# Weight pieces converted in pairs, and the first weight's blocks in two tiles

## The chip, the cores and the metric

The kernel runs on one core of a Trainium2 chip. The core has a matrix engine (TensorE, PE in the profile; PEld is its weight load), a vector engine (VectorE, DVE), a scalar engine (ScalarE, ACT), a general engine (GpSimd, POOL) and a queue engine that issues most transfers (SyncE, SP). Each works through its own instructions in order and waits on semaphores for the others. The metric is the time of one execution on the device in microseconds (us), the median of several runs.

## The reference

Attention without a softmax, normalised per head, then a two-layer feed-forward with a squared relu. The weights `w_in` and `w_out` arrive as 64-bit floats, everything else as 32-bit floats.

```python
kv  = einsum('bhsd,bhse->bhde', k, v)        # 8 x 8 heads, 576 positions, 64 wide
o   = einsum('bhsd,bhde->bhse', q, kv)
x   = o / sqrt(mean(o * o) + 1e-6) * g_norm  # -> (4608 tokens, 512)
r   = maximum(x @ w_in, 0.0)                 # w_in  (512, 2048)
out = (r * r) @ w_out                        # w_out (2048, 512)
```

## The kernel before

Tokens are worked in nine strips of 512. For each strip PE does the up product with `w_in`, then the down product with `w_out`; the attention of later tokens is woven in between. From strip 1 on the products use Strassen's scheme with seven block products (two levels of it further on), so sums and differences of blocks of the weights are needed. Blocks of `w_in` and their sums stay in SBUF; those of `w_out` go to DRAM (`w_out`, `w_deep`) and are streamed back. Only the first three blocks of `w_out` also lie in SBUF (`w_first`: 11, 21 and the sum t1).

The order of the work on each engine is written out by hand: the loop from line 1350 on runs through `steps` and calls transfers, conversions and slices of the attention (`slices`, `attend`) at fixed steps. What the engines are given is in program order, so work of DVE or ACT that is called earlier stands ahead on that engine.

**The conversion.** A weight arrives as 64-bit words and is turned into 32-bit floats with integer arithmetic. There are 32 pieces of 128 x 512 words (512 KB each): 16 of `w_in` (four quarters g, four row chunks kc) and 16 of `w_out`. For each piece ACT does two steps (`convert_on_act`: `w_c` from the upper half of the words, L254; the lower half in place, L258) and DVE four (`conversion`: L266, L268, L272, L275; the last writes the result). Pieces are taken two at a time (`convert_pieces`), the four DVE steps of the two interleaved. ACT is given the steps of the next two pieces before DVE's work on the present two. Then `load_more` has SP issue loads for buffers that come free: `raw` has eight buffers of one piece, `w_c` four.

- `pieces_in` puts pieces of `w_in` at their places; `pieces_out` puts the left half of `w_out`'s columns (blocks 11 and 21) into blocks 4 and 5 of the tile `w_in`.
- `sums_out` converts the right half into two `wt` tiles, which are further buffers of `raw`, forms four differences per tile (L317 to L323, by `minus`, L292) and issues two stores per tile to `w_out` in DRAM (L325), at once.
- `sums_in` scales a quarter on ACT (L301) and forms its block sums on DVE; this is called in the down product of strip 0, by when blocks 4 to 6 no longer hold `w_out`.

The tile `w_in` is [128, 2, 4, 7, 256]: row half, quarter, block, column. Blocks 0 to 3 are the quarters' own, 4 to 6 first `w_out`'s first blocks, later the sums of `w_in`.

**Strip 0.** The first quarter's four pieces are converted step by step between parts of the attention (`first_piece`, with one step on POOL). Then come 16 groups of `up_first` (g, fh, i): four products of 512 columns into one of four PSUM buffers, then a relu and two squares on ACT (L905, L907), which free the buffer. Three of the groups are multiplied early (`first_up`). Conversions are called between the groups: the two pieces with ids 4 and 5 behind group 0, and so on; the four calls of `sums_out` come at the steps 11, 13, 14 and 15. At step 14 blocks 11 and 21 are stored (`store_first`, L333). Then the 14 steps of the down product of strip 0 follow (`down`), which reads the blocks in `w_first`, then streams the others (L954). DVE's sums for it (L886), the normalisation of batch 1 (L490 to L505, L568), the deep sums of the weights (L995, L989) and `sums_in` share DVE; `combine` copies or adds a PSUM bank (L869, L1031) before the bank is used again.

Of the kernel before, what the change touches and what calls it, by code (L numbers as in the profile page):

```python
# [20 lines left out]
def kernel(  # L21
# [34 lines left out]
    nc = tc.nc  # L56
# [36 lines left out]
    raw_pool = conv.enter_context(tc.tile_pool(name="raw", bufs=8))  # L93
    spare_pool = conv.enter_context(tc.tile_pool(name="spare", bufs=1))
    wtmp = conv.enter_context(tc.tile_pool(name="wtmp", bufs=4))
# [113 lines left out]
    def drip_queries():  # L209
# [10 lines left out]
    w_in = wpool.tile([P, KH, NG, 7, WN // 2], FP32, name="w_in")  # L220
# [8 lines left out]
        w_in[:, :, :, b].rearrange("p k g e -> p (k g) e") for b in (4, 5, 6)  # L229
# [3 lines left out]
    sources = [w_in_v[kc, g] for g in range(NG) for kc in range(NP)]  # L233
    sources += [w_out_v[eh, j] for eh in range(2) for j in range(FQ)]
    raw = []

    def load_piece():
        if len(raw) < len(sources):
            t = raw_pool.tile([P, 2, WN // 2], I64, name="raw", tag="raw")
            nc.sync.dma_start(out=t, in_=sources[len(raw)])  # L240
            raw.append(t)
# [4 lines left out]
    words, acted = {}, [0]  # L246

    def convert_on_act(i, parts=(0, 1)):
        view = lambda dt: raw[i].bitcast(dt).rearrange("p b (n two) -> p b n two", two=2)
        low, high, high_f = view(U32)[:, :, :, 0], view(I32)[:, :, :, 1], view(FP32)[:, :, :, 1]  # L250
        r = view(I32)[:, :, :, 0]
        if 0 in parts:
            c = wtmp.tile([P, 2, WN // 2], FP32, name="w_c", tag="w_c")
            nc.scalar.activation(c, high_f, AF.Abs)  # L254
            words[i] = c, r, high

        if 1 in parts:
            nc.scalar.activation(r, low, AF.Copy, scale=2.0**-29)  # L258

    def conversion(i, dest, eng=nc.vector):  # L260

        c, r, high = words.pop(i)
        ci = c.bitcast(I32)


        yield eng.tensor_scalar(out=c, in0=c, scalar1=LEAST, scalar2=MOST, op0=ALU.max, op1=ALU.min)  # L266

        yield nc.vector.tensor_scalar(  # L268
            out=ci, in0=ci, scalar1=3, scalar2=0x3FFFFFFF, op0=ALU.logical_shift_left, op1=ALU.bitwise_and
        )  # L270

        yield nc.vector.scalar_tensor_tensor(  # L272
            out=ci, in0=high, scalar=-(2**30), in1=ci, op0=ALU.bitwise_and, op1=ALU.bitwise_or
        )
        yield nc.vector.tensor_tensor(out=dest.bitcast(I32), in0=ci, in1=r, op=ALU.add)  # L275

    def convert_pieces(ids, dests):

        for i in range(acted[0], min(ids[-1] + 3, len(sources))):
            convert_on_act(i)  # L280
            acted[0] = i + 1
        for _ in zip(*[conversion(i, dest) for i, dest in zip(ids, dests)]):
            pass
        load_more(ids[-1] + 1)
# [8 lines left out]

    def pieces_in(i):
        g, kc = divmod(i, NP)
        b = kc // KH * 2
        convert_pieces((i, i + 1), [w_in[:, kh, g, b : b + 2] for kh in range(KH)])

    def sums_in(g):

        nc.scalar.activation(w_in[:, :, g, 0:4], w_in[:, :, g, 0:4], AF.Copy, scale=g_col)  # L301
        a11, a21, a12, a22, s1, s2, s4 = (w_in[:, :, g, b] for b in range(7))
        nc.vector.tensor_tensor(out=s1, in0=a21, in1=a22, op=ALU.add)
        minus(nc.vector, s2, s1, a11)
        minus(nc.vector, s4, a12, s2)
        minus(nc.vector, a21, a11, a21)

    def pieces_out(j):
        dest = lambda j: w_in[:, j // NG, j % NG, 4:6]
        convert_pieces((NG * NP + j, NG * NP + j + 1), [dest(j), dest(j + 1)])  # L310

    def sums_out(j):
        js = (j, j + 1)
        t = [raw_pool.tile([P, 4, DH], FP32, name="wt", tag="raw") for _ in js]
        convert_pieces([NG * NP + FQ + j for j in js], [x[:, 0:2, :] for x in t])
        for x, j in zip(t, js):
            minus(nc.vector, w_out_t1[:, j, :], x[:, 0], w_out_11[:, j, :])  # L317
        for x, j in zip(t, js):
            minus(nc.vector, x[:, 2], x[:, 1], w_out_t1[:, j, :])
        for x in t:  # L320
            minus(nc.vector, x[:, 0], x[:, 1], x[:, 0])
        for x, j in zip(t, js):
            minus(nc.vector, x[:, 3], w_out_21[:, j, :], x[:, 2])  # L323
            for e in range(2):
                nc.sync.dma_start(out=w_out[3:7, :, e, j].rearrange("b p e -> p b e"), in_=x[:, :, ts(e, P)])  # L325
# [274 lines left out]
    def first_piece(i, n):  # L600

        if i not in first_steps:
            first_steps[i] = conversion(
                i, w_in[:, i % KH, 0, i // KH * 2 : i // KH * 2 + 2], nc.gpsimd if i else nc.vector
            )
        for _ in range(n):
            next(first_steps[i])
# [301 lines left out]
    def up(s, g, p):  # L909
# [5 lines left out]
        for i in range(2):  # L915
            product(p, i, lambda kc: w_in[:, kc, g, A_IN[p], ts(i, P)], lambda kc: rhs[:, :, kc, :], KH)
# [281 lines left out]
    w_half = lambda b, kc, f: w_in[:, kc, 2 * f : 2 * f + 2, b]  # L1198
# [148 lines left out]
    for i in range(NP, NP + 2):  # L1347
        convert_on_act(i)
    acted[0] = NP + 2
# [149 lines left out]
```

## Time and profile before

| | |
|---|---|
| median of 3 runs | 870.89 us (869.28 to 873.78) |
| profiled execution, span from first to last instruction | 867.8 us |
| median less that span | 3.1 us |
| PE busy | 858.3 us, 14176 matmuls |
| DVE busy | 721.5 us, 1236 instructions |
| ACT busy | 352.1 us, 805 instructions |
| POOL busy | 316.2 us, 321 instructions |
| granted clock of PE | 1.000 |

The span is that of the profiled execution; it is the only time of that execution which the page has. An engine's busy time counts instructions that are being carried out; matmuls are pipelined and the end of each is modelled, so a busy PE may have small holes. In a timeline a line gives start, length, engine, line of the code, operation, output and inputs with the shape, a count where several follow each other, and in brackets the idle time before it with the instruction or transfer that ended it.

### The profile page before, as it was taken

Reading aid. Unit: us, or ns where it says so; the run is one execution under the profiler, and the core shown is the slowest. Engines: PE = TensorE matmul, PEld = TensorE weight load, DVE = VectorE, ACT = ScalarE, POOL = GpSimd, SP = SyncE. Lnnn points to the kernel's source line nnn. Section 1 sums busy time; section 2 is a strip of 40 time slices with the busy share of each in tenths; the row PEclk is TensorE's granted clock in tenths of the full one; section 3 lists DMA queues with packets and bytes.
Section 4 is the critical chain, followed back from the end, with each engine's and each line's share of the span. In section 5 each row is a group of like instructions: output and inputs, shape, how many; then the busy total and the mean of one; then the engine's idle time right before and its main releaser. Section 6 shows DMA issues by size and latency. Waiting matters only on the chain.

```text
span 867.8 us, 32590 instructions
## 1 busy us (share of the span) xinstructions
PE 858.3 (99%) x14176; PEld 803.7 (93%) x14176; DVE 721.5 (83%) x1236; ACT 352.1 (41%) x805; POOL 316.2 (36%) x321
## 2 busy tenths in 40 slices
PE   8999999999999999999999999999999999999998
PEld 7445888889999999999999999999999999999998
DVE  3999998879887996789689977897889777975887
ACT  5799251320048303750356034901491148102810
POOL 1100003630459223730574045704470447145700
PEclk9999999999999999999999999999999999999999
DMA  9998997999999997989788979997668856885583
GB/s 312 301 335 251 288 376 233 296 323 361 276 261 261 346 328 235 232 311 336 213 244 272 336 244 258 294 317 260 213 221 300 305 161 220 291 286 195 177 311 124
DMA packets 169470, 236.47 MB, mean 273 GB/s; under 512 B 78704, under 2 KB 133744, under 8 KB 161008
## 3 DMA queue, kind: packets, MB, share of 16 engines
q1 hardware_dynamic: 169024, 234.33, 83.6%
q8 instruction: 111, 1.82, 0.9%
q14 instruction: 31, 0.25, 0.1%
q10 hardware_dynamic: 304, 0.07, 0.0%
HBM read 197.66 MB, written 36.70 MB: 270 GB/s over the span
## 4 chain that ended last, share of the span: by engine, by line
PE 83%; DVE 7%; ACT 5%; DMA 4%; issue 1%; SPq 0%; DVEq 0%; ACTq 0%
PE ps_A L854 35%; PE ps_B L854 31%; PE ps_C L854 5%; PE ps_A L859 4%; PE kv_ps L437 2%; PE x_ps L473 2%; PE ps_B L859 2%; DVE w_t L292 1%; ACT raw L258 1%; ACT w_c L254 1%; DMA w_blk<-w_deep 1%; DMA w_deep<-w_t 1%; DVE wt L292 1%; DMA first_qkv<-in_v_dram 1%; DMA raw<-in_moe_w_out_dram 1%
## 5 line engine op out<-in xcount | busy, mean ns | idle before, releaser
L854 PE MATMUL ps_B<-w_blk,g_s 128*64 128x128 f32 x2016 | 122.0, 273 | 0.0
L854 PEld LDWEIGHTS ps_B<-w_blk,g_s 128*64 128x64 f32 x2016 | 112.6, 137 | 0.1
L854 PE MATMUL ps_A<-x_l,w_in 128*64 128x128 f32 x1568 | 102.4, 273 | 0.6 <-ACT snap L1317 0.6
L292 POOL TENSOR_TENSOR x_l<-xT 128x256 f32<-128x256 f32 x21 | 16.0, 764 | 230.9 <-PE ps_A L854 230.9
L854 PE MATMUL ps_B<-w_blk,gt 128*64 128x128 f32 x1504 | 94.1, 273 | 0.9 <-DMA w_blk<-w_deep 0.9
L854 PE MATMUL ps_A<-w_blk,g_s 128*64 128x128 f32 x1536 | 92.2, 273 | 0.0
L854 PEld LDWEIGHTS ps_A<-x_l,w_in 128*64 128x64 f32 x1568 | 88.9, 137 | 0.9 <-ACT snap L1317 0.8
L1312 POOL TENSOR_TENSOR snap<-snap,gt 128x512 f32<-128x512 f32 x35 | 46.3, 1322 | 112.3 <-ACT snap L1317 102.7
L854 PEld LDWEIGHTS ps_B<-w_blk,gt 128*64 128x64 f32 x1504 | 84.6, 137 | 1.4 <-PE ps_B L854 1.1
L854 PEld LDWEIGHTS ps_A<-w_blk,g_s 128*64 128x64 f32 x1536 | 85.7, 137 | 0.0
L1317 ACT COPY snap<-ps_A 128x512 f32<-128x512 f32 x63 | 36.9, 585 | 103.8 <-PE ps_A L854 96.6
L1252 ACT ACTIVATE gt<-gt 128x512 f32<-128x512 f32 x112 | 70.1, 626 | 9.5 <-DVE gt L1312 9.5
L1253 ACT ACTIVATE gt<-gt 128x512 f32<-128x512 f32 x112 | 70.7, 631 | 3.6
L854 PE MATMUL ps_A<-w_blk,gt 128*64 128x128 f32 x1152 | 71.2, 273 | 0.0
L1101 ACT COPY o_sb<-ps_A 128x128 f32<-128x128 f32 x24 | 6.4, 266 | 144.9 <-PE ps_A L854 115.5
L854 PEld LDWEIGHTS ps_A<-w_blk,gt 128*64 128x64 f32 x1152 | 64.7, 137 | 0.0
L1100 DVE TENSOR_TENSOR o_sb<-o_sb,ps_B 128x256 f32<-128x256 f32 (+1 forms) x123 | 47.4, 386 | 15.0 <-ACT o_sb L1101 9.8
L292 DVE TENSOR_TENSOR gt<-gt 128x2048 f32<-128x2048 f32 (+1 forms) x29 | 59.7, 2063 | 0.0
L1312 POOL TENSOR_TENSOR gt<-gt,snap 128x512 f32<-128x512 f32 x42 | 52.6, 1283 | 15.0 <-DVE snap L1312 15.0
L854 PE MATMUL ps_B<-x_l,w_blk 128*64 128x128 f32 x784 | 51.2, 273 | 0.0
L854 PE MATMUL ps_A<-x_l,w_blk 128*64 128x128 f32 x784 | 51.2, 273 | 0.0
L1101 ACT COPY o_sb<-ps_B 128x128 f32<-128x128 f32 x31 | 8.3, 266 | 96.5 <-PE ps_B L854 96.5
(196 smaller groups left out, 1836.5 us busy)
## 6 DMA issues: line engine op xcount, KB each, us to landing
w_blk<-w_deep SPq DMA_DIRECT2D x56, 1024.0 KB, 7.4
w_blk<-w_out SPq DMA_DIRECT2D x56, 768.0 KB, 6.6
w_blk<-w_in_deep SPq DMA_DIRECT2D x49, 768.0 KB, 5.9
raw<-in_moe_w_in_dram SPq DMA_DIRECT2D x16, 512.0 KB, 7.4
raw<-in_moe_w_out_dram SPq DMA_DIRECT2D x16, 512.0 KB, 4.9
k<-in_k_dram SPq DMA_DIRECT2D x29, 256.0 KB, 5.4
v<-in_v_dram SPq DMA_DIRECT2D x29, 256.0 KB, 6.0
x_d<-x_q SPq DMA_DIRECT2D x27, 256.0 KB, 5.2
```

The lines of the kernel that those rows point to most:

```text
L254: nc.scalar.activation(c, high_f, AF.Abs)
L292: eng.tensor_tensor(out=out, in0=a, in1=b, op=ALU.subtract)
L437: nc.tensor.matmul(ps[ts(h, D), i], lhsT=a, rhs=w, start=i == 0 and c == 0, stop=c == C, skip_group_check=True)
L473: nc.tensor.matmul(ps[half, r, i, ts(p, D)], lhsT=q[row, half], rhs=kvd[b, p][row, row], start=True, stop=True)
L854: nc.tensor.matmul(ps[half], lhsT=lhsT[:, half], rhs=rhs, start=start, stop=stop, skip_group_check=True)
L859: nc.tensor.matmul(bank[BANK[p]][:, i, :], lhsT=lhsT(k), rhs=rhs(k), start=p in (1, 5, 2) and i == 0 and k == 0, stop=k == n - 1, skip_gro ...
L1100: add = lambda out, a, b: nc.vector.tensor_tensor(out=out, in0=a, in1=b, op=ALU.add)
L1101: yield nc.scalar.copy(q[:, 3:4], small(1))
L1252: nc.scalar.activation(o, o, AF.Relu)
L1253: nc.scalar.activation(o, o, AF.Square)
L1312: add = lambda eng, out, a, b: eng.tensor_tensor(out=out, in0=a, in1=b, op=ALU.add)
L1317: nc.scalar.copy(t, ps)
```

## The change

Two pieces that lie side by side share one buffer of `raw` and one of `w_c`, each twice as large and half as many, and every step of ACT and DVE takes both at once (128 x 1024). The first four pieces are still converted one by one, on halves of such buffers. So that the two pieces of a pair lie side by side in the result as well, the chunks of the quarters 1 to 3 are loaded in the order 0, 2, 1, 3. The tile `w_in` keeps four blocks per quarter; the other three, with `w_out`'s first blocks and later the sums, are a tile `w_s`, and `block(b)` chooses between them. `sums_out` uses one tile for two pieces, and its differences, two blocks at a time, and its stores come after the conversion of the following pair (`left_out`); the last two sets come together.

```diff
-    raw_pool = conv.enter_context(tc.tile_pool(name="raw", bufs=8))
+    raw_pool = conv.enter_context(tc.tile_pool(name="raw", bufs=4))
-    wtmp = conv.enter_context(tc.tile_pool(name="wtmp", bufs=4))
+    wtmp = conv.enter_context(tc.tile_pool(name="wtmp", bufs=2))
...
-    w_in = wpool.tile([P, KH, NG, 7, WN // 2], FP32, name="w_in")
+    w_in = wpool.tile([P, KH, NG, 4, WN // 2], FP32, name="w_in")
+    w_s = wpool.tile([P, KH, NG, 3, WN // 2], FP32, name="w_s")
+    block = lambda b: w_in[:, :, :, b] if b < 4 else w_s[:, :, :, b - 4]
...
-    sources = [w_in_v[kc, g] for g in range(NG) for kc in range(NP)]
+    sources = [w_in_v[kc, g] for g in range(NG) for kc in (range(NP) if g == 0 else (0, 2, 1, 3))]
...
     def load_piece():
-        if len(raw) < len(sources):
-            t = raw_pool.tile([P, 2, WN // 2], I64, name="raw", tag="raw")
-            nc.sync.dma_start(out=t, in_=sources[len(raw)])
+        i = len(raw)
+        if i < len(sources):
+            if i % 2 == 0:
+                raw_pairs.append(raw_pool.tile([P, 2, 2, WN // 2], I64, name="raw", tag="raw"))
+            t = raw_pairs[i // 2][:, i % 2]
+            nc.sync.dma_start(out=t, in_=sources[i])
             raw.append(t)
...
+    def act_words(c, view, parts=(0, 1)):
+        low, high_f, r = view(U32)[..., 0], view(FP32)[..., 1], view(I32)[..., 0]
+        if 0 in parts:
+            nc.scalar.activation(c, high_f, AF.Abs)
+        if 1 in parts:
+            nc.scalar.activation(r, low, AF.Copy, scale=2.0**-29)
...
+    def convert_pair_on_act(n):
+        view = lambda dt: raw_pairs[n].bitcast(dt).rearrange("p a b (n two) -> p a (b n) two", two=2)
+        c = wtmp.tile([P, 2, WN], FP32, name="w_c", tag="w_c")
+        act_words(c, view)
+        pair_words[n] = c, view(I32)[..., 0], view(I32)[..., 1]
...
-    def convert_pieces(ids, dests):
-
-        for i in range(acted[0], min(ids[-1] + 3, len(sources))):
-            convert_on_act(i)
+    def convert_pair(n, dest, add_eng=nc.vector):
+
+        for i in range(acted[0], min(n + 2, len(sources) // 2)):
+            convert_pair_on_act(i)
             acted[0] = i + 1
-        for _ in zip(*[conversion(i, dest) for i, dest in zip(ids, dests)]):
-            pass
-        load_more(ids[-1] + 1)
+        deque(conversion(pair_words.pop(n), dest, add_eng=add_eng), 0)
+        load_more(2 * n + 2)
...
     def pieces_in(i):
-        g, kc = divmod(i, NP)
-        b = kc // KH * 2
-        convert_pieces((i, i + 1), [w_in[:, kh, g, b : b + 2] for kh in range(KH)])
+        g, k = divmod(i // 2, KH)
+        convert_pair(i // 2, w_in[:, k, g].rearrange("p (a b) e -> p a (b e)", a=2))
...
     def pieces_out(j):
-        dest = lambda j: w_in[:, j // NG, j % NG, 4:6]
-        convert_pieces((NG * NP + j, NG * NP + j + 1), [dest(j), dest(j + 1)])
+        k, g = divmod(j, NG)
+        convert_pair((NG * NP + j) // 2, side(w_s[:, k, g : g + 2, 0:2]))
+
+    left_out = []
 
     def sums_out(j):
-        js = (j, j + 1)
-        t = [raw_pool.tile([P, 4, DH], FP32, name="wt", tag="raw") for _ in js]
-        convert_pieces([NG * NP + FQ + j for j in js], [x[:, 0:2, :] for x in t])
...
+        x = raw_pool.tile([P, 2, 4, DH], FP32, name="wt", tag="raw")
+        last = j + 2 == FQ
+        convert_pair((NG * NP + FQ + j) // 2, side(x[:, :, 0:2, :]), nc.vector)
+        left_out.append((x, slice(j, j + 2)))
+        while len(left_out) > (0 if last else 1):
+            left_sums(*left_out.pop(0))
+
+    def left_sums(x, js):
+        minus(nc.vector, w_out_t1[:, js, :], x[:, :, 0], w_out_11[:, js, :])
+        minus(nc.vector, x[:, :, 2], x[:, :, 1], w_out_t1[:, js, :])
+        minus(nc.vector, x[:, :, 0], x[:, :, 1], x[:, :, 0])
+        minus(nc.vector, x[:, :, 3], w_out_21[:, js, :], x[:, :, 2])
+        for i in range(2):
             for e in range(2):
-                nc.sync.dma_start(out=w_out[3:7, :, e, j].rearrange("b p e -> p b e"), in_=x[:, :, ts(e, P)])
+                nc.sync.dma_start(out=w_out[3:7, :, e, js.start + i].rearrange("b p e -> p b e"), in_=x[:, i, :, ts(e, P)])
...
-    for i in range(NP, NP + 2):
-        convert_on_act(i)
-    acted[0] = NP + 2
+    convert_pair_on_act(NP // 2)
+    acted[0] = NP // 2 + 1
```

The up product and the sums of `w_in` address their weights by `block(b)` in place of an index into `w_in`; nothing else there is altered.

## The prediction

> **What bounds the kernel now.** I read the page first, then busy time by stage, then the PE timeline, and the ACT and DVE timelines of the stage in which weights are converted (30 to 132 us; the conversion itself ends at 95.4).
>
> ```profile
> PE 858.3 (99%) x14176; PEld 803.7 (93%) x14176; DVE 721.5 (83%) x1236; ACT 352.1 (41%) x805; POOL 316.2 (36%) x321
> PE   8999999999999999999999999999999999999998
> DVE  3999998879887996789689977897889777975887
> ACT  5799251320048303750356034901491148102810
> DMA  9998997999999997989788979997668856885583
> ```
>
> PE is busy nearly everywhere. DVE is full only in slices 2 to 6 (22 to 130 us), ACT in slices 3 and 4, DMA through most of it.
>
> ```profile
> 40.00:50.00 10.00, 10.00 (x24) 4.38 (x24) 10.00 (x23) 9.26 (x19) 0.00 (x0) 1.00 1.11 315
> 50.00:60.00 10.00, 9.71 (x23) 3.94 (x22) 10.00 (x23) 9.56 (x21) 0.00 (x0) 1.00 1.03 377
> 60.00:70.00 10.00, 10.00 (x45) 4.77 (x44) 10.00 (x21) 9.87 (x22) 0.00 (x0) 1.00 0.72 251
> 80.00:95.40 15.40, 15.40 (x159) 11.83 (x158) 15.40 (x40) 8.64 (x20) 0.80 (x1) 1.00 1.04 305
> 95.40:131.80 36.40, 36.14 (x235) 31.31 (x233) 35.30 (x63) 12.78 (x15) 0.00 (x0) 1.00 0.97 340
> ```
>
> After the window come its length, then busy time of PE, PEld, DVE, ACT, POOL, the clock (1.00), DMA share and GB/s. PE, DVE, ACT and DMA are all close to full here: four resources side by side, each with little slack against the others. A busy PE may still be waiting, so I take gaps from start to start.
>
> ```profile
> 37.12 1.88 PE L900 MATMUL ps_A<-xT,w_in 128*128 128x512 f32 x4
> 39.22 1.98 PE L900 MATMUL ps_A<-xT,w_in 128*128 128x512 f32 x4 [0.22 <-DVE w_in L275]
> 51.34 3.60 PE L900 MATMUL ps_A<-xT,w_in 128*128 128x512 f32 x8
> 55.23 3.70 PE L900 MATMUL ps_B<-xT,w_in 128*128 128x512 f32 x8 [0.29 <-ACT gt L907]
> 131.80 7.17 PE L859 MATMUL ps_A<-w_blk,gt 128*128 128x256 f32 x32 [0.26 <-DVE o_sb L1031]
> ```
>
> Eight records take 3.43 us where nothing waits (0.429 each; one product is two). So 37.12 + 4 x 0.429 = 38.84 and the next start, 39.22, leaves 0.39 lost to weights not yet converted; 51.34 + 3.43 = 54.77, so 0.46 lost before 55.23 to ACT, which frees PSUM. Likewise 0.42 before 131.80 (DVE's o_sb), 0.30 before 70.77, and 0.11 to 0.21 at 58.77, 93.12 and 109.61. Together 2.0 us: all that PE can gain in this stage, however fast the other engines get.
>
> ```profile
> 46.92 0.69 ACT L254 ACTIVATE w_c<-raw 128x512 f32<-128x512 f32 x1
> 48.75 0.68 ACT L254 ACTIVATE w_c<-raw 128x512 f32<-128x512 f32 x1 [0.57 <-DMA raw<-in_moe_w_in_dram]
> 50.52 0.66 ACT L907 ACTIVATE gt<-ps_A 128x256 f32<-128x256 f32 x2
> 51.52 0.69 ACT L254 ACTIVATE w_c<-raw 128x512 f32<-128x512 f32 x1 [0.35 <-DMA raw<-in_moe_w_out_dram]
> ```
>
> ACT starts on piece 14 at 46.92 while piece 15 is still under way, and on piece 16 at 51.52; both waits end with a landing.
>
> ```profile
> 75.45 0.75 DVE L292 TENSOR_TENSOR wt<-w_in,wt 128x256 f32<-128x256 f32 x2
> 76.12 0.75 DVE L266 TENSOR_SCALAR w_c<-w_c 128x512 f32<-128x512 f32 x2
> 77.47 1.29 DVE L272 SCALAR_TENSOR_TENSOR w_c<-raw,w_c 128x512 int32<-128x512 int32 x2
> 95.42 2.49 DVE L886 TENSOR_TENSOR g_s<-gt 128x512 f32<-128x512 f32 x4
> ```
>
> Start to start, a 256-wide DVE operation costs 0.335 us and a 512-wide one 0.60; TENSOR_SCALAR at 512 costs 0.335.
>
> **Pairs on DVE.** From 0.335 and 0.60 the fixed part is 0.067 us. A 1024-wide operation is then 1.134; the one 2048-wide row, 2.20 us to the next start, lies on the line. TENSOR_SCALAR at 1024 has no row: 0.602 with the same fixed part, 0.67 if nothing is saved, 1.13 if the wider form ran at the others' rate. I take 0.602, as its operand stays contiguous. A pair is 2 x 0.602 + 2 x 1.134 = 3.47 us against 3.75: 0.28 less for each of 14 pairs, 3.9 us. The block sums go from 32 operations of 256 to 16 of 512, 16 x 0.067 = 1.1 us. DVE loses 5.0 us of work. If the far end (1.13) held, a pair would be 4.54 and the ten pairs before 69.7 would be 8 us late; I hold this unlikely.
>
> **Pairs on ACT.** A 512-wide conversion step costs 0.567 us start to start, the 2048-wide scaling 1.93; by that line 1024 costs 1.02, so 28 steps save 0.11 each, 3.2 us. But one step now needs both pieces landed. Piece 15 was issued at 40.62 and took 8.1 us, landing 48.7; piece 17, issued 45.03, took 7.6, landing 52.7. With DMA share at 1.03 to 1.11 these landings do not move. So pair 7 runs on ACT 48.75 to 50.77 instead of from 46.92 in parts, the group behind it (relu, two squares, 1.18 us) ends at 51.95 instead of 51.1, and PE's group of 51.34 starts at 52.2. Pair 8 starts at 52.75, its group ends at 55.95 against 55.1, and PE's 55.23 becomes 56.1. Pair 9 (landed by 55.2) starts at once. PE is 0.85 us late from here; nothing behind it gives that back but gaps that ACT had caused, some 0.1 to 0.3. Lower end: the landings come earlier by as much and ACT's saving of 1.1 us by then removes the 0.57 of gaps; upper end 1.5, if both pieces were late in turn.
>
> **The order of pieces.** From the second quarter on, a pair is row chunks 0 and 2, then 1 and 3. PE's second product of a group needs the second pair. At 37.12 that matters: pair 2 starts on DVE at 31.7, when its one ACT step is over, ends 35.2, pair 3 ends 38.7; PE stops after one product (37.98) until 38.8, so the gap is 0.83 instead of 0.39. This 0.44 is absorbed in the later start at 52.2. In the two later quarters conversion is done some 4 us before use; uncovered, each would cost up to 0.8.
>
> **Block sums one step later, four buffers.** The sums of a w_out pair and its four stores now follow the conversion of the next pair. The tile of the third pair takes the first one's buffer, so its last conversion step waits for those stores. By the rates above DVE is ready for pair 13 at 71.2, but its ACT step follows three relu groups and copies, as before at 72.2, so DVE starts at 73.1; conversion ends 76.6, the first sums 79.0 (before: 76.1 for these, 79.9 for that conversion). Stores then take, like those issued 75.90 to 77.47 and 82.33 to 83.92, 5.1 to 5.6 us from the first issue to the last landing: 84.2 to 84.7. Three conversion steps end at 81.3, so DVE stands 2.9 to 3.4 us, then needs 1.13 + 2.4 + 3.47 + 2.4 + 2.4: it ends at 96.6 instead of 95.4, 1.2 late. Queued behind it are g_s (PE needs it at 100.57, ready at 97.9: covered), x_n (1.4 us of slack before 104.03) and, through a DVE chain with 0.3 us of holes, o_sb at 131.06, which has no slack. On SP the 16 stores stay in number; the last go out 0.9 to 1.2 later, and the load that reads them (landed 106.4, used 109.6) has 3 us of cover.
>
> **Two tiles.** Strides change, sizes do not: nothing. DMA bytes and issue counts are equal.
>
> **Sum.** PE is 0.85 late by 56 and is held again at 131.8, where DVE's 1.2 lets it start 1.2 later than before. Not additive: about 1.2 with both, less 0.2 of small gaps, +1.0 us. The profiled span of 867.8 becomes 868.8; the 3.1 us between span and median stay, 871.9.
>
> Two sentences of the Trainium skill (Perfetto Trace Analysis, Optimizing Scalar/DVE Operations) pull in opposite directions here: grouping into larger operations can raise throughput on a saturated engine, and breaking instructions up lets work complete sooner where the engine only causes bubbles in others. By the first the time would be rival one's, by the second the forecast's; the rows at 48.75 and 131.80 bear out the second.
>
> **Rivals.** One: the saving carries through. Landings come early enough, the store wait stays under DVE's lead of 2.2 us, and PE closes its gaps: at most -2.0, time 869.0. For it: DVE is full for 65 us and o_sb is late. Against it: the two landings. Two, slower: the stores take the 8.1 us that the w_deep stores of 105 to 108 us took. The last one, issued at 80.65, lands at 88.75, DVE stands 7.4 us, ends 5.2 late, and o_sb passes it on: 875.9. It decides from a stand of 2.2 us on, one for one, and passes 0.5% at 6.6. For it: DMA share 1.04 in 80 to 95 us; against: stores of that very stage took 2.7 to 3.8 at the median. Three: the sums of two blocks are one strided write now; if PE's reads of neighbouring blocks at 83.76 were held for the last such write (96.6), 12.8 us are lost: 883.7. Against: DVE wrote one such block at 92.74 while a strided store of another, issued at 88.20 for 7.3 us, was still under way.
>
> **How the numbers follow.** Forecast 0.52, rival one 0.22, two 0.14, three 0.03, unnamed shifts of later loads (one load now costs PE 1.1 us at 288) 0.09. Half a percent, 4.35 us, is about what a measurement can tell from no change. PE's gaps forbid more than -2.0 here, so faster is 0.06 for unnamed causes; slower holds three, most of two and some unnamed, 0.17. The range runs from rival one less the runs' own scatter (868.4) to rival two (876.2). The forecast by itself spans 870.2 (the landings cost nothing, the stores do) to 873.6 (both ends of these costs). The three runs before span 4.5 us, which is more than the forecast's step.
>
> **What would show it.** Right: 128x1024 rows at 1.1 to 1.3 us on DVE, ACT pair steps at 48.75 and 52.75, PE starts at 52.2 and 56.1, and DVE idle about 3 us before the third L275 into wt, ended by a w_out store. Wrong: no such idle time, DVE's end before 94, or a PE gap near 84.

## The result, and the profile after

The changed kernel takes 875.39 us (median, 873.52 to 880.19) against 869.98 us (868.49 to 873.78) for the kernel before, run beside it: a ratio of 1.0062, with a 95% interval of 1.0047 to 1.0077. It is slower by 5.4 us. In its profiled execution the span is 872.5 us, 4.7 more than the 867.8 of before. Of the page of the changed kernel, busy time by engine and the rows by slice:

```profile
PE 859.9 (99%) x14176; PEld 804.5 (92%) x14176; DVE 719.6 (82%) x1164; ACT 349.2 (40%) x777; POOL 315.2 (36%) x321
PE   8999999999999999999999999999999999999998
DVE  3898999779967996889788976897889777875897
ACT  5779251230047502660357024911491147102810
DMA  9997998999999997989797979998677956885483
```

DVE carries out 72 instructions fewer and is busy for 1.9 us less, and ACT too does the same work in less time: read by busy time alone, the change is a small success. The windows of the same kernel (length; busy time of PE, PEld, DVE, ACT, POOL; clock, DMA share, GB/s) tell another story:

```profile
80.00:95.40 15.40, 15.40 (x158) 11.37 (x157) 11.95 (x16) 8.94 (x19) 0.10 (x1) 1.00 1.07 320
95.40:131.80 36.40, 33.88 (x224) 29.20 (x223) 35.29 (x63) 13.31 (x16) 0.00 (x0) 1.00 0.94 330
```

From 80 to 95.4 us DVE was busy without a break before; now it is idle for 3.45 us of them. In the window behind that PE is busy for 2.26 us less than before. The PE timeline of the changed kernel at its new holes:

```profile
39.42 2.84 PE L919 MATMUL ps_A<-xT,w_in 128*128 128x512 f32 x6 [1.73 <-DVE w_in L290]
53.05 3.70 PE L919 MATMUL ps_A<-xT,w_in 128*128 128x512 f32 x8 [0.48 <-ACT gt L926]
106.57 1.31 PE L662 MATMUL xt_ps<-ident,x_n 128*128 128x128 f32 x8 [0.90 <-DVE x_n L587]
114.03 2.21 PE L878 MATMUL ps_A<-w_blk,gt 128*128 128x256 f32 x9 [1.60 <-DVE gt L306]
136.09 7.17 PE L878 MATMUL ps_A<-w_blk,gt 128*128 128x256 f32 x32
```

(The lines of the code have moved: L281, L283, L287, L290 are the four steps that were L266, L268, L272, L275; L306 is `minus`, L926 the squares, L587 `x_n`, L878 the products of the down stage.) Taken from start to start as before, the holes are 1.89 us before 39.42, 0.65 before 53.05, 0.62 before 57.10, 1.06 before 106.57 and 1.8 before 114.03. The start that was at 131.80, where PE waited for DVE's `o_sb`, is at 136.09, just behind the same sum (135.35 to 136.03 on DVE). The ACT timeline of the changed kernel, at the steps that the prediction spoke of:

```profile
49.60 1.15 ACT L257 ACTIVATE w_c<-raw 128x1024 f32<-128x1024 f32 x1 [3.75 <-DMA raw<-in_moe_w_in_dram]
53.66 1.16 ACT L257 ACTIVATE w_c<-raw 128x1024 f32<-128x1024 f32 x1 [0.67 <-DMA raw<-in_moe_w_out_dram]
```

And the DVE timeline of the changed kernel, one whole pair, then the place where DVE stands, then its first sum for the down product:

```profile
39.28 0.69 DVE L281 TENSOR_SCALAR w_c<-w_c 128x1024 f32<-128x1024 f32 x1
40.00 0.69 DVE L283 TENSOR_SCALAR w_c<-w_c 128x1024 int32<-128x1024 int32 x1
40.73 1.23 DVE L287 SCALAR_TENSOR_TENSOR w_c<-raw,w_c 128x1024 int32<-128x1024 int32 x1
42.09 1.23 DVE L290 CUSTOM_DVE_ANT_0 w_in<-raw,w_c 128x2048 uint16<-128x2048 uint16 x1
43.23 0.69 DVE L281 TENSOR_SCALAR w_c<-w_c 128x1024 f32<-128x1024 f32 x1
...
82.79 1.23 DVE L287 SCALAR_TENSOR_TENSOR w_c<-raw,w_c 128x1024 int32<-128x1024 int32 x1
87.16 1.23 DVE L290 CUSTOM_DVE_ANT_0 wt<-raw,w_c 128x2048 uint16<-128x2048 uint16 x1 [3.14 <-DMA w_out<-wt]
...
99.85 2.49 DVE L905 TENSOR_TENSOR g_s<-gt 128x512 f32<-128x512 f32 x4
```

Two things are to be seen. A pair takes 39.28 to 43.23, 3.95 us, where the two pieces in turn took 3.75 before: the wide form is slower. And DVE stands for 3.14 us at 87.16 until the delayed stores have left the buffer. `g_s` starts at 99.85 instead of 95.42, 4.43 us later, and from there nothing is made up: `x_n` 105.83 (before 101.41), `o_sb` 135.35 (before 131.06), the first product of strip 1 on PE 143.10 (before 138.81), the end 4.7 later.

**Where the 4.43 us come from.** I cut DVE's time up to `g_s` in three, from PE's first wait for converted weights (24.86 before, 24.41 after; the profiles differ by up to 2.4 us in what lies ahead of it, so I count from there): up to the start of pair 3; from there to the start of pair 12, which is nine pairs; and the last four pairs with all sums and stores. Before, these are 11.08, 33.75 and 25.73 us; after, 10.91, 35.59 and 28.94. So -0.17, +1.84 (nine times 0.20) and +3.21 (3.14 of it is the stand), less 0.45 for the earlier opening: 4.43. The same cut serves for all experiments.

**PE's own lateness.** The early holes are less than that. Counted from the same wait, PE's first product with `gt` starts 58.90 us later before (83.76) and 60.83 after (85.24), so by then PE is 1.93 us late, while DVE is 4.88 late at `g_s` and strip 1 is 4.74 late. PE makes up the difference standing: it waits for DVE before 106.57 and 114.03.

### The profile page after: what moved, and what is told of

It is laid out like the page before. It is cut to its first block, busy times and chain, and to the rows that moved or that the text cites. A ratio compares the mean times of both kernels' runs of the same rounds, so it can differ in the third digit from the quotient of the medians.

```text
span 872.5 us, 32448 instructions
## 1 busy us (share of the span) xinstructions
PE 859.9 (99%) x14176; PEld 804.5 (92%) x14176; DVE 719.6 (82%) x1164; ACT 349.2 (40%) x777; POOL 315.2 (36%) x321
## 4 chain that ended last, share of the span: by engine, by line
PE 78%; DVE 10%; DMA 7%; ACT 3%; SPq 1%; issue 1%; DVEq 0%
PE ps_A L873 33%; PE ps_B L873 29%; PE ps_C L873 5%; PE ps_A L878 4%; DMA w_blk<-w_deep 3%; PE kv_ps L456 2%; PE x_ps L492 2%; PE ps_B L878 2%; DVE w_t L306 1%; DVE w_c L287 1%; DMA w_blk<-w_in_deep 1%; DMA w_blk<-w_out 1%; DVE wt L306 1%; DVE gt L306 1%; PE ps_C L878 1%
## 5 line engine op out<-in xcount | busy, mean ns | idle before, releaser
L306 POOL TENSOR_TENSOR x_l<-xT 128x256 f32<-128x256 f32 x21 | 16.3, 775 | 230.5 <-PE ps_A L873 230.5
L306 DVE TENSOR_TENSOR gt<-gt 128x2048 f32<-128x2048 f32 (+1 forms) x29 | 59.6, 2063 | 0.0
L873 PE MATMUL ps_A<-x_l,w_in 128*64 128x128 f32 x896 | 58.5, 273 | 0.0
L873 PEld LDWEIGHTS ps_A<-x_l,w_in 128*64 128x64 f32 x896 | 50.8, 137 | 0.1
```

Of the source, the lines that this page charges most:

```text
L306: eng.tensor_tensor(out=out, in0=a, in1=b, op=ALU.subtract)
L873: nc.tensor.matmul(ps[half], lhsT=lhsT[:, half], rhs=rhs, start=start, stop=stop, skip_group_check=True)
```

## The experiments

Theory: two DVE costs make up the loss, the slower wide step and the stand for the stores; ACT's pairs, the order and the two tiles cost nothing that lasts. Rival: the late landings, to which ACT's pairs are bound, hold PE from 53 us on, and DVE's part is hidden. A second question was why a wide step is slow: by its width or because each step reads what the one before wrote.

All times in us. "Pair 3", "nine pairs" and "last four" are the three stretches, "g_s" their sum against before, "strip 1" the first product of strip 1, counted from the same wait, against before (113.95). The ratio is that of medians to the kernel before, with its 95% interval. Single runs of one kernel differ by several us, so a place in a trace settles a delay better than a median does. Behind the start of strip 1 the profiled executions take between 729.0 us (before) and 735.5 (halves_in_turn), in no order that follows the edits (731.7 in split_alone); the cause stays open, and it may be why medians and places differ. The rows from the third on stand in the order of the sections below.

| kernel | pair 3 | nine pairs | last four | g_s | strip 1 | ratio |
|---|---|---|---|---|---|---|
| before | 11.08 | 33.75 | 25.73 | 0 | 0 | 1 |
| after | 10.91 | 35.59 | 28.94 | +4.88 | +4.74 | 1.0062 (1.0047 to 1.0077) |
| sums_at_once | 10.90 | 35.59 | 26.41 | +2.34 | +2.66 | 1.0042 (1.0022 to 1.0061) |
| halves_in_turn | 10.70 | 34.36 | 29.18 | +3.68 | +3.53 | 1.0062 (1.0038 to 1.0085) |
| both_undone | 10.70 | 35.51 | 25.61 | +1.26 | +3.34 | 1.0039 (1.0018 to 1.0060) |
| tiles_alone | 11.05 | 33.75 | 25.61 | -0.15 | +0.26 | 1.0020 (1.0003 to 1.0037) |
| delay_alone | 11.05 | 33.75 | 29.37 | +3.61 | +3.47 | 1.0051 (1.0033 to 1.0068) |
| wide_alone | 11.57 | 43.98 | 31.04 | +16.03 | +19.33 | 1.0226 (1.0202 to 1.0250) |
| act_and_order_undone | 11.57 | 43.96 | 35.31 | +20.28 | +20.16 | 1.0235 (1.0215 to 1.0256) |
| one_after_other | 11.20 | 42.37 | 29.53 | +12.54 | +12.41 | 1.0162 (1.0139 to 1.0186) |
| wide_new_order | 11.55 | 35.59 | 26.44 | +3.02 | +3.30 | 1.0052 (1.0032 to 1.0073) |
| act_undone | 11.55 | 35.59 | 29.78 | +6.36 | +6.24 | 1.0096 (1.0068 to 1.0124) |
| mixed | 11.06 | 33.75 | 28.53 | +2.78 | +3.18 | 1.0040 (1.0014 to 1.0066) |
| split_alone | 11.05 | 33.75 | 25.74 | -0.02 | +0.18 | 1.0000 (0.9982 to 1.0017) |

### The sums at once

The changed kernel, with the differences and stores of each pair right behind its conversion.

```diff
-        while len(left_out) > (0 if last else 1):
+        while left_out:
```

> The changed kernel, but the block sums of a w_out pair and its stores follow its own conversion at once. Theory (two costs on DVE: the wait of the third wt tile for the first one's stores, 3.0 us, and 0.2 us more per pair because a wide step waits for the one before it): the 3.1 us of idle time before the third L290 into wt goes, DVE ends its last block sum near 96.9 us instead of 99.9, and the time falls by 2.5 to 3.0 us against the changed kernel: ratio to before 1.0025 to 1.0035. Rival (the early holes of PE at 39, 53 and 57 us decide, DVE's late end is covered): no more than 0.5 us, ratio 1.0055 or above.

DVE doesn't stand for the stores any more and the last stretch falls from 28.94 to 26.41, 2.53 us less. It isn't back at 25.73: the first sum now reads what the last conversion step has just written and starts 1.26 us behind it (80.45 to 81.71) in place of 1.14, and the pairs are still slow. So the stand is a real cost of 2.5 us on the path to strip 1, where 2.1 us of it arrive. `g_s` comes at 97.44 and the ratio is 1.0042, both somewhat above what was expected.

### DVE's steps on the halves in turn

The changed kernel, but DVE takes each of the four steps on the first piece, then on the second, 512 wide.

```diff
-        deque(conversion(pair_words.pop(n), dest, add_eng=add_eng), 0)
+        of = pair_words.pop(n)
+        for _ in zip(*[conversion(tuple(x[:, a] for x in of), dest[:, a], add_eng=add_eng) for a in range(2)]):
+            pass
```

> The changed kernel with ACT's steps in pairs as they are, but DVE's four steps on the two halves of a pair in turn, 512 wide. Theory (a wide step stands waiting for the one before it): a pair falls from 3.95 to 3.75 us on DVE, the hole of PE at 39 us shrinks below 1.0 us, DVE's end comes 2.0 to 2.4 us earlier with the wait for the stores still about 3 us, ratio 1.003 to 1.004. Rival (the wide steps are slower in themselves, or ACT's landings set DVE's pace): pairs stay at 3.9 or above in places and the ratio stays above 1.005.

The DVE timeline, one pair from its first step to that of the next, then the stand:

```profile
39.03 0.75 DVE L281 TENSOR_SCALAR w_c<-w_c 128x512 f32<-128x512 f32 x2
42.78 0.75 DVE L281 TENSOR_SCALAR w_c<-w_c 128x512 f32<-128x512 f32 x2
...
86.27 1.29 DVE L290 CUSTOM_DVE_ANT_0 wt<-raw,w_c 128x1024 uint16<-128x1024 uint16 x2 [3.06 <-DMA w_out<-wt]
```

A pair takes 3.75 us again, with twice the instructions on the same bytes. The nine pairs take 34.36, not 33.75, since DVE is now early enough to wait for ACT, 0.31 us at 54.63 for one. DVE also stands 0.83 us for ACT at 74.29. The stand for the stores remains (3.06 us at 86.27). `g_s` gains 1.2 us against the changed kernel; the median shows none of it (1.0062, where 1.003 to 1.004 was expected).

### Both undone

The two edits above together.

> The two edits together: sums at once and DVE's steps on halves in turn. What is left of the change is ACT in pairs, the order of the chunks, the buffers in pairs, 512-wide sums and the two tiles. Theory: both DVE costs are gone, DVE ends near 94.8, PE keeps only what ACT's later start costs it (0.5 to 0.9 us at 52 to 57): ratio 1.000 to 1.001. Rival (the early holes decide): 1.002 or more.

The last stretch is as before (25.61). What is left lies in the middle: DVE waits for ACT 0.40 us at 40.73 and 1.06 at 53.13, and ACT had waited 3.66 us for a landing at 51.97. So with DVE back at its speed, ACT's pairs do cost something: their late landings reach DVE. PE also has a hole of 0.87 us before 39.79, which goes with the new order, and one of 2.58 before 55.35:

```profile
55.35 3.70 PE L921 MATMUL ps_A<-xT,w_in 128*128 128x512 f32 x8 [2.42 <-ACT gt L928]
```

Counted from its first wait, PE is 2.68 us late at its first product with `gt` (87.39) and, with no wait in between, still 2.61 late at 128.03 (124.47 before). DVE stands 2.12 us at 120.23 for stores of `w_deep`, and PE then 0.98 before 136.09 for `o_sb`. By my estimate PE alone would have put strip 1 some 2.2 us late without that stand (128.03 and the 6.94 that the same product takes in tiles_alone). So where DVE is only 1.26 us late the early holes decide, as the rival had it, and the ratio of 1.0039 is the rival's (1.002 or more), not the theory's. Stands of 0.31 to 0.45 us for the same stores are in sums_at_once, tiles_alone, wide_new_order and mixed; why this one is longer stays open.

### The tiles alone

Both undone, and besides ACT converts piece by piece and the chunks come in the old order. What remains of the change are the buffers of two pieces, the block sums at 512, and the two tiles.

```diff
-        act_words(c, view)
+        for a in range(2):
+            act_words(c[:, a], lambda dt: view(dt)[:, a])
...
-    sources = [w_in_v[kc, g] for g in range(NG) for kc in (range(NP) if g == 0 else (0, 2, 1, 3))]
+    sources = [w_in_v[kc, g] for g in range(NG) for kc in range(NP)]
...
-        g, k = divmod(i // 2, KH)
-        convert_pair(i // 2, w_in[:, k, g].rearrange("p (a b) e -> p a (b e)", a=2))
+        g, kc = divmod(i, NP)
+        b = kc // KH * 2
+        convert_pair(i // 2, w_in[:, :, g, b : b + 2].rearrange("p k b e -> p k (b e)"))
```

> In addition ACT takes the two pieces of a pair one by one and the chunks are loaded in the old order. Only buffers that hold two pieces, the 512-wide sums and the two tiles are left. Theory: as before, ratio 0.999 to 1.0005. Rival (buffers that come free in pairs, or the second tile, cost something): 1.002 or more.

All three stretches are as before to 0.12 us, and strip 1 starts 0.26 us later at most. The last stretch also shows what the wider block sums are worth: 0.12 us over four pairs, where I had counted 1.1. The ratio of 1.0020 leaves 1.7 us, of which the stages up to strip 1 show only 0.3; where the rest lies stays open.

### The later sums alone

As the kernel above, but with the sums behind the next pair, as the change has them.

> Of the change only the later sums (with buffers in pairs and two tiles): DVE's steps on halves in turn, ACT piece by piece, the old order of chunks. Theory: DVE stands about 3 us before the third conversion into wt, ended by a w_out store; g_s comes 2 to 3 us after 95.4, PE starts strip 1 2 to 3 us after 138.8. Ratio about 1.003. Rival (the wait needs the slower wide steps ahead of it): idle below 1 us, g_s within 0.5 us of 95.4.

```profile
86.15 1.29 DVE L291 CUSTOM_DVE_ANT_0 wt<-raw,w_c 128x1024 uint16<-128x1024 uint16 x2 [3.24 <-DMA w_out<-wt]
```

DVE stands 3.24 us at 86.15 and the last stretch is 3.64 us longer; the other two are as before. (DVE also stands 0.70 us for ACT at 74.33.) This arrives at PE: holes of 1.14 us before 105.43 (`x_n`) and 1.8 before 112.89, and strip 1 is 3.47 us late, more than the 2 to 3 expected. The later sums alone thus make the kernel slower.

### Wide steps alone, in the old order

As the tiles alone, but DVE's steps 1024 wide. In the old order the two chunks of a pair lie in different row halves, so the last step writes `w_in[:, 0:2, g, b : b + 2]`, two stretches with the other quarters' blocks between them.

> Of the change only DVE's 1024-wide steps (with buffers in pairs and two tiles): ACT takes the pieces one by one, the chunks are loaded in the old order, the sums follow at once. Theory (a step waits for the one before it): a pair takes 3.95 us on DVE, 0.2 more than before, so DVE's first g_s comes 1.5 to 2.2 us after the 95.4 of before, PE starts strip 1 as much later (138.8 before), and no store is waited for. Ratio about 1.002. Rival (wide steps cost nothing when ACT feeds them piece by piece): g_s at 95.4 or earlier.

Something quite different decides this kernel. Its PE timeline (L921 is the up product, L291 here the last conversion step):

```profile
43.64 4.28 PE L921 MATMUL ps_C<-xT,w_in 128*128 128x512 f32 x6 [9.77 <-DVE w_in L291]
47.76 1.02 PE L921 MATMUL ps_A<-xT,w_in 128*128 128x512 f32 x2
54.99 5.43 PE L921 MATMUL ps_A<-xT,w_in 128*128 128x512 f32 x6 [6.21 <-DVE w_in L291]
```

The group at 43.64 reads only the first quarter, whose conversion ended long before; yet it is held until a result of the third quarter is written (L291 from 42.36 to 43.59). In return DVE stands 1.87 us at 48.05 for a product that doesn't read what it is about to write. The waits fit a rule by which a write in two stretches counts for everything from its first to its last byte; that rule is inferred from who waits for whom, and no run isolates it. Behind these waits the granted clock is low as well: 0.64 from 43.64 to 47.76 and 0.50 from 54.99 to 60.26, where six records take 4.12 and 5.27 us from start to start, against 2.57 for six at full clock. The run does show what the new order of chunks is for: with it, a pair's result is one stretch and these waits are gone (wide_new_order, below).

### ACT and the order undone

The changed kernel with ACT piece by piece and the old order, that is wide steps and late sums.

> The changed kernel with ACT piece by piece and the old order of the chunks; the wide DVE steps and the later sums stay. Theory (DVE's late end decides): the holes of PE at 53 and 57 us shrink, yet g_s still comes near 99.5 and strip 1 starts near 142.7, as in the changed kernel (99.85 and 143.1); ratio 1.005 to 1.006. Rival (the early holes add to the rest): strip 1 starts 1.5 us or more earlier, below 141.6, ratio 1.004 or less.

The same false waits (9.95 us before 44.32, 6.38 before 55.65) and the stand for stores behind them, 2.1 us now. The run says no more about ACT; for that the order has to stay, as in the next but one.

### One piece after the other, in the kernel before

The kernel before, but DVE ends the four steps of a piece before it takes the next. Width, buffers, order and sums stay.

```diff
-        for _ in zip(*[conversion(i, dest) for i, dest in zip(ids, dests)]):
-            pass
+        for i, dest in zip(ids, dests):
+            deque(conversion(i, dest), 0)
```

> The kernel before with one edit: DVE's four steps of a piece are issued one after the other, then those of the next piece, instead of in turn. Same instructions, same sizes, same buffers. Theory (a step that reads what the step before it wrote starts 0.1 to 0.2 us later than one that doesn't): two pieces take 4.5 to 4.8 us instead of 3.75; with 12 pairs in the full stretch DVE's g_s comes 8 to 11 us after 95.4 and the ratio is 1.008 to 1.012. Rival (what cost time in the changed kernel was width, not dependence): pairs stay at 3.75 us, ratio 1.000.

This settles why a wide step is slow. The DVE timeline of this kernel, one piece:

```profile
54.85 0.42 DVE L266 TENSOR_SCALAR w_c<-w_c 128x512 f32<-128x512 f32 x1
55.30 0.43 DVE L268 TENSOR_SCALAR w_c<-w_c 128x512 int32<-128x512 int32 x1
55.76 0.69 DVE L272 SCALAR_TENSOR_TENSOR w_c<-raw,w_c 128x512 int32<-128x512 int32 x1
56.59 0.69 DVE L275 CUSTOM_DVE_ANT_0 w_in<-raw,w_c 128x1024 uint16<-128x1024 uint16 x1
57.20 0.42 DVE L266 TENSOR_SCALAR w_c<-w_c 128x512 f32<-128x512 f32 x1
```

Same instructions, same width, only another order: from start to start 0.45, 0.46, 0.83 and 0.61, where in turns they take 0.335, 0.335, 0.60 and 0.60. A step that reads what the one just before wrote starts only after its end (0.03 us after a TENSOR_SCALAR, 0.14 after the SCALAR_TENSOR_TENSOR), while an independent one starts 0.08 to 0.09 us before that end. That makes 0.12, 0.12 and 0.23 per piece, two pieces 4.71 us. The last step, followed by another piece, costs what it did. The wide pair has the same gaps, 0.12, 0.13 and 0.23 above my line, once instead of twice: 3.47 + 0.48 = 3.95. What the change saves in fixed cost (0.28) is less than what the lost interleaving costs (0.48). `g_s` is 12.54 us late here, more than the 8 to 11 expected, as the nine pairs of the full stretch and the last four all pay the 0.96 (13 x 0.96 = 12.5).

The rows for this stood in the trace of before, where the first pieces are converted one by one. Its DVE timeline:

```profile
25.52 0.42 DVE L268 TENSOR_SCALAR w_c<-w_c 128x512 int32<-128x512 int32 x1
25.97 0.69 DVE L272 SCALAR_TENSOR_TENSOR w_c<-raw,w_c 128x512 int32<-128x512 int32 x1
26.80 0.69 DVE L275 CUSTOM_DVE_ANT_0 w_in<-raw,w_c 128x1024 uint16<-128x1024 uint16 x1
```

0.45 and 0.83 from start to start: the price of a dependent step. I had taken the prices of 0.335 and 0.60 from rows in which two pieces alternate.

The Trainium skill (VectorE: DVE Perf Modes, The DRAIN you can't avoid) says that a read of what the instruction before wrote needs a semaphore even on the same engine, and that one instruction in between does as well. The traces show a price for the first, 0.83 against 0.60, and none for the second; that it is the price of a semaphore they don't show. The same section of the Trainium skill says of a chain of copies that a semaphore after each costs nothing extra; that doesn't carry over to these dependent steps. The Trainium skill (VectorE: DVE Perf Modes, The TRN2 errata) says that one large tile pays the fixed cost once and many small ones each time. The traces agree between like steps: 1.14 against two times 0.60 where they are independent, 1.36 against two times 0.83 where they are dependent. The pair as a whole went the other way because the change turned independent steps into dependent ones.

### Wide steps alone, in the new order

ACT piece by piece and sums at once; wide steps and the new order stay.

> DVE's 1024-wide steps once more without the later sums, now with the changed kernel's order of the chunks, so that a pair's result lies in one piece; ACT takes the pieces one by one. Theory (dependence alone, 0.12 + 0.12 + 0.23 us per pair on top of the 3.47 of the sizes): pairs of 3.95 us, no hole of PE near 34 or 49 us, first g_s at 97 to 97.8, strip 1 at 140.3 to 141.2, ratio 1.001 to 1.0035. Rival (the 20 us of the run with the old order belong to the wide steps, not to their strided result): holes of 6 to 10 us again, ratio 1.02.

No false waits. The nine pairs take 35.59, exactly as in the changed kernel, +1.84. The start of pair 3 is 0.47 us late: the first wide step needs both pieces of `w_c`, and ACT, piece by piece, gives out the second one only as its third step, so that DVE waits 1.55 us at 31.25 (0.92 in the changed kernel). PE, which waits for the wide steps, has a hole of 2.51 us before 39.30, and behind it the granted clock is 0.61 from 39.30 to 43.68: six records take 4.38 us there, 2.68 in the changed kernel. `g_s` is 3.02 us late, PE at its first product with `gt` 2.89, strip 1 3.30, so PE and DVE come about equally late. The median is 0.5% above before, more than the 0.35% expected at most: the wide steps alone, with ACT piece by piece, make the kernel slower, too.

### ACT undone

The changed kernel with ACT piece by piece, nothing else.

> The changed kernel with one edit: ACT takes the two pieces of a pair one by one. Theory (DVE's late end decides, ACT's later start at pairs 7 and 8 is covered by it): PE's holes at 53 and 57 us shrink below 0.3 us in sum, yet g_s stays at 99.3 to 99.9, strip 1 starts at 142.4 to 143.1, ratio 1.005 to 1.006. Rival (these holes add): strip 1 at 141.9 or earlier.

I had expected nothing of it, and the rival a gain; it is slower than the changed kernel, by 1.5 us at `g_s` and strip 1. DVE waits 1.55 us at 31.87 and 0.74 at 76.21, each for ACT's second `w_c`, then 3.14 at 88.51 for the stores as before. The holes of PE at 53 and 57 are gone (its groups start at 51.05, 54.48 and 57.91, without a gap), but the one at 39 has grown from 1.89 to 2.53, and the granted clock behind it is 0.62 from 39.94 to 44.18:

```profile
39.94 4.41 PE L920 MATMUL ps_A<-xT,w_in 128*128 128x512 f32 x6 [2.36 <-DVE w_in L291]
```

The six records take 4.24 us from start to start, 2.68 in the changed kernel. So PE is not earlier but later at its first product with `gt` (2.76 us, 1.93 in the changed kernel), and the run doesn't test whether the holes at 53 and 57 add. That early holes don't add here shows otherwise: in both kernels strip 1 is late by what DVE is late at `g_s` (6.24 and 6.36; 4.74 and 4.88), not by that and PE's own lateness, because PE waits for DVE further on. With wide DVE steps ACT's pairs are a gain.

### Wide steps interleaved with the sums

An attempt at a better version: old order, DVE's halves in turn, ACT piece by piece; only in `sums_out` the steps are wide, with a difference of the pair before between each two.

```diff
+            for step, _ in enumerate(conversion(of, dest, add_eng=add_eng)):
+                for _ in range((1, 1, 2, 0)[step]):
+                    next(between)
```

> A version meant to be faster: ACT piece by piece, the old order, DVE on halves in turn, and in the w_out sums the four wide steps of a pair in turn with the four wide sums of the pair before it, so that no step follows the one it reads, and the stores have one more step to land. Theory: about 1.2 us less DVE work than before, no wait for a store, g_s at 94.2, strip 1 at 138.4 to 138.8: PE has so little to gain that the ratio is 0.998 to 1.001. Rival (the third tile still waits for the stores): idle over 1 us before the third conversion into wt, g_s after 95.4.

```profile
75.02 0.70 DVE L282 TENSOR_SCALAR w_c<-w_c 128x1024 f32<-128x1024 f32 x1 [1.92 <-ACT w_c L257]
75.63 0.69 DVE L315 TENSOR_TENSOR w_s<-wt,w_s 128x512 f32<-128x512 f32 x1
76.23 0.69 DVE L284 TENSOR_SCALAR w_c<-w_c 128x1024 int32<-128x1024 int32 x1
76.84 0.69 DVE L315 TENSOR_TENSOR wt<-wt,w_s 128x512 f32<-128x512 f32 x1
77.44 1.22 DVE L288 SCALAR_TENSOR_TENSOR w_c<-raw,w_c 128x1024 int32<-128x1024 int32 x1
```

The interleaving does what it should: a wide step and a difference in turn start every 0.60 to 0.61 us, without the extra 0.12. No wait for stores is left either. But the first wide step now needs both pieces of `w_c`, and DVE stands for ACT: 1.92 us at 75.02, where ACT is busy with relus and copies until 73.2, and 2.37 at 89.26, where ACT itself has waited 4.30 us at 87.34 for a piece of `w_out` whose load went out at 82.15, behind the stores. The last stretch is 2.80 us longer than before. No version tried here is faster than the kernel before.

### The two tiles in the kernel before

The kernel before, with blocks 4 to 6 in a tile of their own.

```diff
-    w_in = wpool.tile([P, KH, NG, 7, WN // 2], FP32, name="w_in")
+    w_in = wpool.tile([P, KH, NG, 4, WN // 2], FP32, name="w_in")
+    w_s = wpool.tile([P, KH, NG, 3, WN // 2], FP32, name="w_s")
+    block = lambda b: w_in[:, :, :, b] if b < 4 else w_s[:, :, :, b - 4]
```

> The kernel before with the two tiles w_in and w_s and nothing else of the change. Theory (strides only): g_s at 95.4, strip 1 at 138.8 as before, ratio 0.9985 to 1.0015. Rival (the layout itself costs PE or the sums something, as the run with only tiles, buffers and sums hinted at with 1.002): ratio 1.002 or more.

1.0000, and all three stretches equal to 0.03 us. The tiles cost nothing.

**What the experiments add up to.** At `g_s`, the later sums alone cost 3.61 us and the wide steps alone (with the order) 3.02; both together, without ACT's pairs, 6.36, close to the sum of 6.63. ACT's pairs take 1.5 off this, which leaves the 4.88 of the changed kernel. For the changed kernel the theory of two DVE costs stands: the two together make DVE later than PE's early holes make PE. That ACT's pairs and the order cost nothing that lasts was wrong in both directions: ACT's pairs help where DVE's steps are wide, and where they aren't (both_undone) DVE loses 1.26 us with them and PE 2.68, which then decides.

## Why the prediction was right or wrong

- **What bounds the kernel.** Right: with 2.0 us to gain on PE and DVE, ACT and DMA full beside it, every delay of DVE showed. The direction was right; the size was not: +1.0 us was forecast, +4.7 came in the span and +5.4 in the median. That 875.39 lies within the range is luck: the forecast by itself spanned 870.2 to 873.6, and the range reached further only for rival two, whose slow stores didn't come.
- **Pairs on DVE.** This is the step that failed, the price of a pair of pieces on DVE. A pair was to take 3.47 us and took 3.95; the term that was to give 0.28 a pair costs 0.20. My prices came from alternating rows and were applied to a chain in which each step reads the one before. The line itself held where a step is independent (1.14 measured, 1.134 computed). My bound "nothing is saved" for TENSOR_SCALAR, 0.67, was also below the 0.73 measured, so the term's likely range was too narrow on the side that counted, and I set aside the far end without a row for dependent steps.
- **Block sums.** 1.1 us were to be saved. A set of sums takes 2.54 us where it took 2.68 and 2.41 was forecast, since one of the four follows the one that it reads (0.72 against 0.60). Where the set comes right behind its conversion, as in tiles_alone, its first sum also follows the step that it reads, and 0.12 us over four pairs is what is left.
- **Stand for the stores.** Right: forecast 2.9 to 3.4 us, ended by a `w_out` store; measured 3.14. The stores took 5.55 us from the first issue (81.45) to the last landing (87.00), where I had 5.1 to 5.6. But the work on both sides of it was costed with the wrong price. Pair 13 starts at 74.86 instead of 73.1, the three steps ahead of the stand end 9.2 us after that instead of 8.2, and what follows the stand takes 12.7 instead of 11.8. That makes `g_s` 99.85 instead of 96.6.
- **Pairs on ACT.** Right in kind: ACT waits for the landing at 49.60 and 53.66 (48.75 and 52.75 forecast), and PE starts at 53.05 and 57.10 (52.2 and 56.1). The 0.8 us on top come from pair 3, whose buffer came free at 39.37, and with it the issue of pieces 14 and 15 (40.65 and 41.27 in place of 39.23 and 40.62). I had taken this for the main loss of the path. It is covered by DVE's later one: PE is 1.93 us late at its first product with `gt`, strip 1 4.74. And I missed that a wide DVE step needs ACT's pairs.
- **The order of pieces.** The gap came as described but measured 1.89 us, not 0.83, as pair 3 ended at 39.37 and not at 38.7, and PE came to it 0.45 us earlier. What I didn't see is that the wide steps need this order: in the old one strip 1 is 16.0 us later (wide_alone against wide_new_order) or 13.9 (act_and_order_undone against act_undone).
- **Two tiles.** Right: 1.0000.
- **DVE's chain without slack.** Right, and this is why the size of the DVE term mattered so much: 4.43 us at `g_s` are 4.29 at `o_sb` and 4.29 at strip 1.
- **The rivals.** One fell with the DVE term. Two's time, 875.9, is near what came, but not its mechanism: the four stores that DVE stood for took 3.3 to 3.9 us each, not 8.1, and the stand was 3.14, not 7.4. Three didn't happen, there is no gap near 84; but its mechanism, a write in several stretches that holds readers of other blocks, is the likely one in wide_alone, at another place.

## What to carry to other kernels

Before you widen instructions, see whether their neighbours are independent: two chains in turn hide what each step pays after the one before, and one chain of double width can be slower though it has half the instructions and less busy time. Take prices from start to start, and from rows in the same relation (dependent or not) as the new code will have. When work that frees a buffer is moved behind other work, count the stores' whole way to their landing as a wait of the one who needs the buffer.

## What the runs showed that I hadn't expected

- A DVE step that reads the result of the instruction just before costs 0.12 us more after a TENSOR_SCALAR or a TENSOR_TENSOR and 0.23 more after a SCALAR_TENSOR_TENSOR on integers, at 512 and at 1024 columns alike (0.45 against 0.335 and 0.83 against 0.60; 0.73 and 1.36 against 0.602 and 1.134 on the line). With one unrelated instruction between them nothing is added.
- A wide write in two stretches held PE for 9.94 and 6.37 us for blocks that it didn't touch, by the look of the waits.
- An early hole of PE costs nothing when a later wait for another engine takes it in (the changed kernel: PE 1.93 us late at its first product with `gt`, DVE 4.88 at `g_s`, strip 1 4.74), and decides when the other engine comes in time (both_undone: 2.68, 1.26 and 3.34).
- Behind holes of 2.51 and 2.53 us the granted clock was 0.61 and 0.62 for 4.38 and 4.24 us (wide_new_order, act_undone), which made PE's next six records 1.7 and 1.56 us longer; behind one of 2.58 us (both_undone) it stayed at 1.00. What decides this no run shows.
